# Two chunks of batch 1 instead of one are stored last with one-hot MoE rows; the second is computed among the last MoE stages

## The chip, the cores and the metric

The kernel runs on one core of one Trainium2 chip. The metric is the time of one execution on the device in microseconds. The kernel before took 265.82 us, the median of 12 runs (265.46 to 266.96). PE is the matrix engine, DVE the vector engine, ACT the scalar engine, POOL the GpSimd engine and SP the engine that only issues transfers here. PSUM is the memory that PE writes its results to; SBUF is the working memory.

## The reference

Inputs are q, k and v, each of 4 batches x 6208 rows x 256 columns, float32. The first half is an attention over columns (cross covariance), the second a mixture of depths (MoE): in each batch the 128 rows with the highest scores go through a small network and are replaced.

```
qn = q / (norm(q, axis=1) + 1e-6);  kn = k / (norm(k, axis=1) + 1e-6)
a  = softmax(kn.T @ qn / tau)           # 256 x 256 per batch, over the last axis
x  = v @ a                              # 6208 x 256 per batch
scores = x @ w_gate
for each batch b:
    top = the 128 rows of x[b] with the largest scores
    ye  = relu(x[b, top] @ w1) @ w2     # 256 -> 1024 -> 256
    g   = 1 / (1 + exp(-scores[b, top]))
    out[b, top] = x[b, top] + g * ye    # all other rows of out are x
```

The norm of every column needs all rows of q and k, so no row of the output of a batch can be computed before that batch's q and k have been read. The MoE rows of a batch are known only when all its scores are.

## The kernel before

**Tiling.** A batch is cut into six chunks of 1024 rows (0 to 5) and a rest of 64. A chunk lies in SBUF as 128 partitions x 8 rows x 256 columns. POOL's queue loads q, k and v, turning them to bf16 on the way. Batches are called by number, 0 to 3. In the code `H` is batch 1, `E` is batch 2 and `L` is batch 3.

**Stages of a batch.** `p1_steps` multiplies the rows of k with q into `s_ps` and collects the squares in `g_ps`. `softmax_stages` makes the 256 x 256 matrix `a_sb`, and a pair of columns `aw_sb`, with which scores can be had without x. Then, in groups of four rows of each partition, `p2_transpose` (op "T") transposes v into `vt_sb`, `p2_score` (op "S") adds the scores, and `p2_out` (op "O") multiplies with `a_sb` into a PSUM bank, two rows at a time, which ACT (late in the kernel also DVE) copies into an SBUF tile called `stage`. When a chunk's `stage` is full, `emit_store` issues a 1 MB store on SP's queue. `select_stages` finds the 128 rows by a search in seven steps on DVE and PE, and POOL gathers those rows of v by an indirect transfer (`vg`). `mlp_stages` transposes `vg`, forms the rows of x (`xe`), transposes them, runs the hidden layer (`h_sb`, 16 matmuls) and the output layer (8 matmuls), and makes the new rows, `upd`, on DVE. POOL then writes these 128 rows into the output by an indirect transfer, the scatter. It has to come behind the stores of the same batch, since it overwrites some of their rows, and it waits until they have landed.

**The order of the work.** The order of instructions on each engine is written out by hand: `plan` lists the operations, and generators for the softmax, the selection and the MoE (`smx_side`, `side`, `side2`) are advanced one stage at a time between them, by an estimate of the time spent (`spent`, `SLOT_US`). Output of batch b is computed among the first stage of batch b + 1. The last batch has no successor. While its q and k are loaded, batch 2's scores are computed and four groups of its output. Stores of batch 2, and those of batch 1's chunks 3 and 4 (`HOLD`), are held back in `deferred` and issued behind the last loads, by `flush_deferred`. Then come the rest of batch 2's output and batch 3's output, with batch 3's selection and batch 2's MoE between the pairs (`between`).

**A chunk that is stored last.** Batch 1's chunk 5 is treated otherwise. Its groups get only their scores in the usual place; their transposed rows wait in `vt_late`. Its output is computed between batch 3's softmax stages by `late_pair`, four times, two rows at a time. Each row takes two matmuls with `a_sb` and three more that add the MoE rows of that batch: a one-hot matrix made by `late_onehot` (which partition holds which chosen row) is multiplied with `late_parts`, the MoE's addition cut into three bf16 parts that sum to the float32 value. This chunk's store may thus come after batch 1's scatter. It is the last on SP's queue, issued behind all of batch 3's.

**The end.** After all output, the last MoE (batch 3's) runs by itself, behind 24 matmuls without a use for their result (`keep_warm`):

```
    emit_store(H, NFULL - 1)
    ...
    while waiting:
        side2.append(mlp_stages(waiting.pop(0)))
    keep_warm(24)
    while side2:
        advance(side2)
```

**Buffers.** There are seven `stage` tiles, so a chunk held back takes one away from the others. Most tiles of the MoE exist once or twice (`bufs`). PSUM banks are taken in turn by `out_psum`.

Of the kernel before, what the change touches and what calls it, by code (L numbers as in the profile page):

```python
# [9 lines left out]
F32 = mybir.dt.float32  # L10
BF16 = mybir.dt.bfloat16
# [3 lines left out]
ALU = mybir.AluOpType  # L15
AX = mybir.AxisListType

P = 128
RPP = 8
# [7 lines left out]
def kernel(  # L27
# [73 lines left out]
    gs = [g for ci in range(NFULL + 1) for g in groups(ci)]  # L101
    E = B - 2
    H = B - 3
    late = [(NFULL - 1, 0, 4), (NFULL - 1, 4, 4)]

    def mixed(b, ci, extra):

# [195 lines left out]
    def softmax_stages(b):  # L303
        s_ps, g_ps = acc[b]
        s_sb = smx.tile([P, 2, C], F32, name="s_sb")
        nc.scalar.copy(s_sb, s_ps)  # L306
        junk = smx.tile([P, P], F32, name="junk")
        nsq = smx.tile([P, 4], F32, name="nsq")
        for i in range(4):
            nc.vector.tensor_tensor_reduce(out=junk, in0=g_ps[:, i, :], in1=ident_f, scale=1.0,  # L310
                                           scalar=0.0, op0=ALU.mult, op1=ALU.add,
                                           accum_out=nsq[:, i:i + 1])


        y0 = smx.tile([P, 4], F32, name="y0")
        nc.vector.tensor_scalar(out=y0.bitcast(I32), in0=nsq.bitcast(I32), scalar1=-0.5,
                                scalar2=float(0x5F1FFFF9), op0=ALU.mult, op1=ALU.add)
        t0 = smx.tile([P, 4], F32, name="t0")
        nc.vector.tensor_tensor(out=t0, in0=nsq, in1=y0, op=ALU.mult)
        nc.vector.scalar_tensor_tensor(out=t0, in0=t0, scalar=-0.703952253, in1=y0, op0=ALU.mult,  # L320
                                       op1=ALU.mult)
        y1 = smx.tile([P, 4], F32, name="y1")
        nc.vector.scalar_tensor_tensor(out=y1, in0=t0, scalar=0.703952253 * 2.38924456, in1=y0,
                                       op0=ALU.add, op1=ALU.mult)
        x1 = smx.tile([P, 4], F32, name="x1")
        nc.vector.tensor_tensor(out=x1, in0=nsq, in1=y1, op=ALU.mult)
# [25 lines left out]
        a_sb = a_pool.tile([P, 2, C], BF16, name="a_sb")  # L352
        aw_sb = a_pool.tile([P, 2, 2], BF16, name="aw_sb")
        for cc in range(2):
            r = smx.tile([P, 1], F32, name=f"r{cc}")
            nc.vector.tensor_scalar_add(r, rsum[:, cc:cc + 1], 1e-9)
            nc.vector.reciprocal(r, r)
            nc.vector.tensor_scalar_mul(a_sb[:, cc, :], e[:, cc, :], r)
            awj = smx.tile([P, C], BF16, name="awj")
            nc.vector.tensor_tensor_reduce(out=awj, in0=a_sb[:, cc, :], in1=wg_bcast, scale=1.0,  # L360
                                           scalar=0.0, op0=ALU.mult, op1=ALU.add,
                                           accum_out=aw[:, cc:cc + 1])

        nc.vector.tensor_copy(aw_sb[:, :, 0], aw)
        nc.vector.tensor_tensor(out=aw_sb[:, :, 1], in0=aw, in1=aw_sb[:, :, 0], op=ALU.subtract)
        a_tiles[b] = (a_sb, aw_sb)
# [3 lines left out]
    stage_of = {}  # L370
    deferred = []
    gate_done = []
    held = {b: NFULL + 1 - (b == H) for b in range(B)}
    side = []
    side2 = []
    waiting = []
# [19 lines left out]
    def p2_transpose(b, g, on_act=False):  # L396
        ci, s0, n = g
        parts = P if ci < NFULL else REM
        vt = loaded[("v", b, ci)][0]
        vt_ps = vt_psum()  # L400
        for j in range(n):
            for cc in range(2):
                nc.tensor.transpose(vt_ps[:, cc, j, :parts], in_=vt[:parts, s0 + j, cc * P:(cc + 1) * P],  # L403
                                    identity=ident_b[:parts, :parts])
        if b == H and g in late:
            vt_sb = moe.tile([P, 2, 4, P], BF16, name="vt_late", bufs=2)
        else:
            vt_sb = vt_pool.tile([P, 2, 4, P], BF16, name="vt_sb")
        if on_act:
            nc.scalar.copy(vt_sb[:, :, :n, :parts], vt_ps[:, :, :n, :parts])  # L410
        else:
            nc.vector.tensor_copy(vt_sb[:, :, :n, :parts], vt_ps[:, :, :n, :parts])  # L412
        return vt_sb
# [74 lines left out]
    def late_pair(k):  # L488


        g = late[k // 2]
        onehot, parts = late_moe
        if k == 0:
            stage_of[(H, NFULL - 1)] = st_pool.tile([P, RPP, C], F32, name="stage")
        st = stage_of[(H, NFULL - 1)]
        a_sb = a_tiles[H][0]
        o_ps = out_psum()
        row = g[1] + k % 2 * 2
# [20 lines left out]

    def late_onehot(idx):  # L520

        base = float(H * N + (NFULL - 1) * CHUNK)
        at = moe.tile([P, 1], F32, name="late_at")
        nc.vector.tensor_copy(at, idx)
        nc.vector.tensor_scalar(out=at, in0=at, scalar1=-base, scalar2=1.0 / RPP, op0=ALU.add, op1=ALU.mult)
        at_row = moe.tile([P, RPP], F32, name="late_at_row")
        nc.vector.tensor_scalar(out=at_row, in0=iota_row[:, 0:RPP], scalar1=-1.0 / RPP, scalar2=at,
                                op0=ALU.mult, op1=ALU.add)
        onehot = moe.tile([P, RPP, P], BF16, name="late_onehot")
        nc.vector.tensor_tensor(out=onehot, in0=iota_row[:, None, :].to_broadcast([P, RPP, P]),  # L530
                                in1=at_row[:, :, None].to_broadcast([P, RPP, P]), op=ALU.is_equal)
        late_moe.append(onehot)

    def emit_store(b, ci):
# [13 lines left out]
    def select_stages(b):  # L548
# [85 lines left out]
        nc.vector.tensor_scalar(out=idx, in0=mps[:, NCOL + 2:NCOL + 3], scalar1=fl, scalar2=toff,  # L634
                                op0=ALU.max, op1=ALU.add)
        yield
        vg = moe.tile([P, C], BF16, name="vg", bufs=3)
        nc.gpsimd.indirect_dma_start(out=vg, out_offset=None, in_=v_flat,
                                     in_offset=bass.IndirectOffsetOnAxis(ap=idx[:, 0:1], axis=0))

# [5 lines left out]
    def mlp_stages(b):  # L646
# [2 lines left out]
        tp = ps_vt.tile([P, 2, 4, P], BF16, name="vt_ps")  # L649
        for cc in range(2):  # L650
            nc.tensor.transpose(tp[:, cc, 0, :], in_=vg[:, cc * P:(cc + 1) * P], identity=ident_b)
        vgt = moe.tile([P, 2, P], BF16, name="vgt", bufs=2)
        nc.vector.tensor_copy(vgt, tp[:, :, 0, :])
        yield
        mps = ps_m.tile([P, 512], F32, name="m_ps")
# [1 line left out]
            nc.tensor.matmul(mps[:, 0:C], lhsT=vgt[:, cc, :], rhs=a_sb[:, cc, :], start=cc == 0,  # L657
                             stop=cc == 1)
        xe = moe.tile([P, D], F32, name="xe", bufs=2)
        xe_b = moe.tile([P, D], BF16, name="xe_b", bufs=2)  # L660
        nc.vector.tensor_copy(xe_b, mps[:, 0:D])
        nc.vector.tensor_copy(xe, mps[:, 0:D])
        yield
        tp = ps_vt.tile([P, 2, 4, P], BF16, name="vt_ps")
        for dc in range(2):
            nc.tensor.transpose(tp[:, dc, 0, :], in_=xe_b[:, dc * P:(dc + 1) * P], identity=ident_b)
        xet = moe.tile([P, 2, P], BF16, name="xet", bufs=2)
        nc.vector.tensor_copy(xet, tp[:, :, 0, :])
        scj = moe.tile([P, D], BF16, name="scj")
        ssc = moe.tile([P, 1], F32, name="ssc")  # L670
        nc.vector.tensor_tensor_reduce(out=scj, in0=xe, in1=wg_bcast, scale=1.0, scalar=0.0, op0=ALU.mult,
                                       op1=ALU.add, accum_out=ssc)
        gate = moe.tile([P, 1], F32, name="gate", bufs=2)
        nc.scalar.activation(gate, ssc, AF.Exp, scale=-1.0)
        nc.vector.tensor_scalar_add(gate, gate, 1.0)
        nc.vector.reciprocal(gate, gate)
        yield
        h_sb = moe.tile([P, NFC, P], BF16, name="h_sb", bufs=2)
        for hf in range(NFC // 4):
            h_ps = out_psum().rearrange("p a c -> p (a c)")  # L680
            for f4 in range(4):
# [165 lines left out]
        do_out(E, op[2], False)  # L847
    for g in gs[-1:] + gs[:-1]:
        do_out(b, g, False)
    emit_store(H, NFULL - 1)  # L850
    while side:
        advance(side)
    while side2:
        advance_all(side2)
    while waiting:
        side2.append(mlp_stages(waiting.pop(0)))
    keep_warm(24)
    while side2:
        advance(side2)

# [34 lines left out]
```

## Time and profile before

| what | value |
|---|---|
| median of 12 runs | 265.82 us |
| the profiled execution's own time | 266.29 us |
| its span (first to last instruction) | 264.5 us |
| PE / DVE / ACT / POOL busy, share of the span | 76% / 46% / 31% / 21% |
| mean granted clock of PE | 0.94 |
| chain that ended last, by engine | DMA 59%, PE 16%, issue 11%, DVE 9% |
| DMA packets of the core | 66.97 MB, mean 253 GB/s |
| 1 MB stores, issue to landing (median of 24) | 8.9 us |
| scatters, issue to landing (median of 4) | 6.8 us |
| second to last and last scatter, start | 244.92 and 254.97 us |

Times inside the kernel are counted from the span's start. The span is shorter than the execution's time by what lies around it. The granted clock is the share of its full rate that PE got from its throttle. A row like `L477 PE MATMUL o_ps<-a_sb,vt_sb` names the line, the engine, the operation, and what is written from what. In the timeline the first two columns are the start and the time in which the row's instructions ran, and `xN` is how many they are; in brackets stands how long the engine had been idle and what ended that. In the chain of waits, each piece is an instruction, a transfer in flight (DMA), or time in which nothing that the profile shows was waited for ("issue"). `POOLq` and `SPq` are the sequencers of POOL and SP.

### The profile page before, as it was taken

How to read it: one execution, taken by the hardware profiler on the slowest of the kernel's cores; microseconds unless marked ns; L12 is line 12 of the kernel's file. 1: busy time of each engine (PE TensorE's matmuls, PEld its weight loads, DVE VectorE, ACT ScalarE, POOL GpSimd, SP SyncE). 2: the span in 40 equal slices, each digit the busy share in tenths (PEclk: the TensorE clock that was granted, in tenths of full speed). 3: DMA queues.
4: the chain of work that ended last, by engine and by line, in shares of the span. 5: the costliest groups of instructions: out<-in, count | busy, mean ns of one | idle time of the engine just before them, and what ended most of it. 6: DMA issues, size and time to landing. Idle time of an engine off the chain costs nothing.

```text
span 264.5 us, 6087 instructions
## 1 busy us (share of the span) xinstructions
PE 200.0 (76%) x2584; PEld 176.2 (67%) x2584; DVE 121.2 (46%) x464; ACT 81.7 (31%) x146; POOL 55.4 (21%) x104
## 2 busy tenths in 40 slices
PE   0096768899937677699986886899999799799700
PEld 0086656789926566589975785898988688578500
DVE  0200002614403366713438785773975827868400
ACT  3102000167720000118731000434102866795200
POOL 7113123121110023221301233320422003010110
PEclk9999999999977799799998899999999999999855
DMA  6999999999999999999999999999999989999960
GB/s 221 227 229 225 216 210 214 214 212 283 320 317 317 296 213 213 214 214 208 313 315 248 213 212 224 211 215 213 214 209 213 213 278 398 409 392 403 422 252 0
DMA packets 17642, 66.97 MB, mean 253 GB/s; under 512 B 2000, under 2 KB 4688, under 8 KB 14544
## 3 DMA queue, kind: packets, MB, share of 16 engines
q0 software_dynamic: 12384, 38.93, 73.7%
q1 hardware_dynamic: 5232, 27.66, 26.4%
q8 instruction: 20, 0.33, 0.4%
q14 instruction: 6, 0.05, 0.0%
HBM read 79.04 MB, written 25.95 MB: 397 GB/s over the span
## 4 chain that ended last, share of the span: by engine, by line
DMA 59%; PE 16%; issue 11%; DVE 9%; POOL 1%; ACT 1%; POOLq 1%; DVEq 0%; SPq 0%
DMA k_ch<-in_k_dram 26%; DMA v_ch<-in_v_dram 17%; DMA q_ch<-in_q_dram 13%; PE o_ps L477 5%; DMA out_dram<-stage 3%; PE s_ps L291 2%; PE vt_ps L403 2%; DVE cnt L588 2%; DVE cmp L584 2%; PE sc_ps L431 1%; PE g_ps L295 1%; PE g_ps L293 1%; DVE stage L483 1%; PE g_ps L477 1%; PE m_ps L595 1%
## 5 line engine op out<-in xcount | busy, mean ns | idle before, releaser
L291 PE MATMUL s_ps<-q_ch,k_ch 128*128 128x256 bf16 x384 | 95.1, 288 | 32.3 <-DMA k_ch<-in_k_dram 31.7
L293 PE MATMUL g_ps<-q_ch 128*128 128x128 bf16 x384 | 87.8, 229 | 1.1 <-DVE nsq L310 1.0
L295 PE MATMUL g_ps<-k_ch 128*128 128x128 bf16 x384 | 87.8, 229 | 0.0
L291 PEld LDWEIGHTS <-k_ch 128*128 128x128 bf16 x384 | 39.6, 103 | 37.8 <-DMA k_ch<-in_k_dram 34.9
L477 PE MATMUL o_ps<-a_sb,vt_sb 128*128 128x256 bf16 x298 | 43.9, 271 | 1.9 <-ACT vt_sb L410 1.3
L295 PEld LDWEIGHTS <-k_ch 128*128 128x128 bf16 x384 | 39.7, 103 | 8.0 <-issue 1.6
L485 ACT COPY stage<-o_ps 128x512 f32<-128x512 f32 x68 | 38.3, 590 | 15.5 <-PE o_ps L477 15.4
L293 PEld LDWEIGHTS <-q_ch 128*128 128x128 bf16 x384 | 39.6, 103 | 1.0 <-issue 0.6
L412 DVE COPY vt_sb<-vt_ps 128x1024 bf16<-128x1024 bf16 (+1 forms) x33 | 20.8, 633 | 31.7 <-PE vt_ps L403 31.6
L477 PEld LDWEIGHTS <-vt_sb 128*128 128x128 bf16 (+1 forms) x376 | 29.4, 97 | 8.1 <-issue 4.4
L403 PE MATMUL vt_ps<-ident_b,v_ch 128*128 128x128 bf16 x336 | 24.6, 219 | 1.8 <-DMA v_ch<-in_v_dram 0.7
L431 PEld LDWEIGHTS <-vt_sb 128*128 128x128 bf16 (+1 forms) x376 | 23.8, 96 | 2.5 <-DVE sc L552 0.2
L306 ACT COPY s_sb<-s_ps 128x512 f32<-128x512 f32 x4 | 2.3, 585 | 73.6 <-PE s_ps L291 43.0
L403 PEld LDWEIGHTS <-v_ch 128*128 128x128 bf16 x384 | 22.2, 97 | 4.0 <-DMA v_ch<-in_v_dram 3.0
L174 POOL DMA_DIRECT2D q_ch<-in_q_dram x23 | 12.7, 553 | 57.9 <-PE g_ps L295 35.9
L431 PE MATMUL sc_ps<-aw_sb,vt_sb 128*128 128x2 bf16 (+1 forms) x376 | 24.1, 164 | 0.0
L310 DVE CUSTOM_DVE_ANT_0 junk<-g_ps,ident_f 128x128 f32<-128x128 f32 x16 | 4.6, 290 | 38.7 <-PE g_ps L295 38.3
L174 POOL DMA_DIRECT2D v_ch<-in_v_dram x24 | 12.8, 538 | 25.0 <-DMA q_ch<-in_q_dram 12.2
L174 POOL DMA_DIRECT2D k_ch<-in_k_dram x23 | 12.5, 543 | 25.4 <-DMA k_ch<-in_k_dram 7.6
L588 DVE TENSOR_REDUCE cnt<-cmp 128x7 bf16<-128x343 bf16 x28 | 14.4, 513 | 1.0
L410 ACT COPY vt_sb<-vt_ps 128x1024 bf16<-128x1024 bf16 x11 | 10.6, 1012 | 13.1 <-PE vt_ps L403 13.1
L584 DVE SCALAR_TENSOR_TENSOR cmp<-u,delta,shares 128x343 bf16<-128x343 f32 x24 | 13.9, 579 | 0.9
(156 smaller groups left out, 215.0 us busy)
## 6 DMA issues: line engine op xcount, KB each, us to landing
out_dram<-stage SPq DMA_DIRECT2D x24, 1024.0 KB, 8.9
v_ch<-in_v_dram POOLq DMA_DIRECT2D x24, 512.0 KB, 14.8
q_ch<-in_q_dram POOLq DMA_DIRECT2D x23, 512.0 KB, 16.9
k_ch<-in_k_dram POOLq DMA_DIRECT2D x23, 512.0 KB, 17.9
stage<-in_moe_w_dram SPq DMA_DIRECT2D x2, 1024.0 KB, 23.4
q_ch<-in_q_dram POOLq DMA_DIRECT2D x2, 256.0 KB, 9.6
k_ch<-in_k_dram POOLq DMA_DIRECT2D x2, 256.0 KB, 9.7
out_dram<-stage_rem SPq DMA_DIRECT2D x4, 64.0 KB, 20.5
```

The source lines that it names most:

```text
L174: ins = nc.gpsimd.dma_start(out=t, in_=view(src, b, ci))
L291: nc.tensor.matmul(s_ps[:, cc, :], lhsT=ks[:, sl], rhs=qs, start=first and cc == 0, stop=last and cc == 1)
L293: nc.tensor.matmul(g_ps[:, cc, :], lhsT=qs[:, sl], rhs=qs[:, sl], start=first and cc == 0, stop=False)
L295: nc.tensor.matmul(g_ps[:, 2 + cc, :], lhsT=ks[:, sl], rhs=ks[:, sl], start=False, stop=last and cc == 1)
L403: nc.tensor.transpose(vt_ps[:, cc, j, :parts], in_=vt[:parts, s0 + j, cc * P:(cc + 1) * P], identity=ident_b[:parts, :parts])
L410: nc.scalar.copy(vt_sb[:, :, :n, :parts], vt_ps[:, :, :n, :parts])
L412: nc.vector.tensor_copy(vt_sb[:, :, :n, :parts], vt_ps[:, :, :n, :parts])
L431: nc.tensor.matmul(sc_ps[:parts, col, :], lhsT=vt_sb[:, cc, j, :parts], rhs=aw_sb[:, cc, :], start=cc == 0 and col in (0, NCOL - 1), stop= ...
L477: nc.tensor.matmul(o_ps[:parts, pj, :], lhsT=vt_sb[:, cc, j, :parts], rhs=a_sb[:, cc, :], start=pj == 0 and cc == 0, stop=pj == m - 1 and ...
L485: nc.scalar.copy(st[:parts, s0 + pair * 2:s0 + pair * 2 + m, :], o_ps[:parts, :m, :])
L584: nc.vector.scalar_tensor_tensor(out=cmp, in0=wide, scalar=delta, in1=thr, op0=ALU.subtract, op1=ALU.is_ge)
L588: nc.vector.tensor_reduce(out=cnt, in_=cmp, axis=AX.X, op=ALU.add)
```

## The change

Batch 1's chunks 4 and 5 are now both treated as chunk 5 was. Their four groups get only scores in their usual place among batch 2's first stage, and chunk 4 is no longer in the list of stores held back. `late_onehot` makes two one-hot matrices. The four `late_pair` operations between batch 3's softmax stages now compute chunk 4, and its store is issued where that of chunk 5 was. Chunk 5 is computed in the last MoE: two pairs in place of the `keep_warm` matmuls, one after the stage that makes `xe`, one after the hidden layer; its store follows. To make room, several tiles lose a buffer, and some results that nobody reads share one.

```diff
-    late = [(NFULL - 1, 0, 4), (NFULL - 1, 4, 4)]
+    LATE = [NFULL - 2, NFULL - 1]
+    late = [(ci, s0, 4) for ci in LATE for s0 in (0, 4)]
...
-        junk = smx.tile([P, P], F32, name="junk")
+        junk = smx.tile([P, P], BF16, name="junk")
...
-            awj = smx.tile([P, C], BF16, name="awj")
+            awj = smx.tile([P, C], BF16, name="junk_row")
...
-    held = {b: NFULL + 1 - (b == H) for b in range(B)}
+    held = {b: NFULL + 1 - (len(LATE) if b == H else 0) for b in range(B)}
...
-            vt_sb = moe.tile([P, 2, 4, P], BF16, name="vt_late", bufs=2)
+            vt_sb = moe.tile([P, 2, 4, P], BF16, name="vt_late", bufs=len(late))
...
-        onehot, parts = late_moe
-        if k == 0:
-            stage_of[(H, NFULL - 1)] = st_pool.tile([P, RPP, C], F32, name="stage")
-        st = stage_of[(H, NFULL - 1)]
+        onehots, parts = late_moe
+        onehot = onehots[:, LATE.index(g[0]), :, :]
+        if g[1] == 0 and k % 2 == 0:
+            stage_of[(H, g[0])] = st_pool.tile([P, RPP, C], F32, name="stage")
+        st = stage_of[(H, g[0])]
...
-        onehot = moe.tile([P, RPP, P], BF16, name="late_onehot")
-        nc.vector.tensor_tensor(out=onehot, in0=iota_row[:, None, :].to_broadcast([P, RPP, P]),
-                                in1=at_row[:, :, None].to_broadcast([P, RPP, P]), op=ALU.is_equal)
+        onehot = moe.tile([P, len(LATE), RPP, P], BF16, name="late_onehot")
+        for i in range(len(LATE)):
+            at_row = moe.tile([P, RPP], F32, name=f"late_at_row{i}")
+            nc.vector.tensor_scalar(out=at_row, in0=iota_row[:, 0:RPP], scalar1=-1.0 / RPP, scalar2=at,
+                                    op0=ALU.mult, op1=ALU.add)
+            nc.vector.tensor_tensor(out=onehot[:, i, :, :], in0=iota_row[:, None, :].to_broadcast([P, RPP, P]),
+                                    in1=at_row[:, :, None].to_broadcast([P, RPP, P]), op=ALU.is_equal)
+            if i + 1 < len(LATE):
+                nc.vector.tensor_scalar(out=at, in0=at, scalar1=-float(P), scalar2=None, op0=ALU.add)
...
-        vg = moe.tile([P, C], BF16, name="vg", bufs=3)
+        vg = moe.tile([P, C], BF16, name="vg", bufs=2)
...
-        h_sb = moe.tile([P, NFC, P], BF16, name="h_sb", bufs=2)
+        h_sb = moe.tile([P, NFC, P], BF16, name="h_sb")
...
-    emit_store(H, NFULL - 1)
+    emit_store(H, LATE[0])
     while side:
         advance(side)
     while side2:
         advance_all(side2)
-    while waiting:
-        side2.append(mlp_stages(waiting.pop(0)))
-    keep_warm(24)
+    late_pair(4)
+    late_pair(5)
+    side2.append(mlp_stages(waiting.pop(0)))
+    advance(side2)
+    advance(side2)
+    late_pair(6)
+    advance(side2)
+    advance(side2)
+    late_pair(7)
+    emit_store(H, LATE[1])
     while side2:
         advance(side2)
```

`vgt`, `xe_b`, `xet` and `gate` also go from two buffers to one, like `h_sb`, and `scj` shares the tile `junk_row` with `awj`. The instructions of POOL keep their order. On PE, some stages of the selection and the MoE stand one or two steps later among the matmuls of batch 2's and batch 3's first stage, since less time is counted as spent before them.

More of the change, by code (lines that the diff above doesn't have):

```diff
@@ L520, in late_onehot @@
     def late_onehot(idx):
-        base = float(H * N + (NFULL - 1) * CHUNK)
+        base = float(H * N + LATE[0] * CHUNK)
         at = moe.tile([P, 1], F32, name="late_at")
@@ L525, in late_onehot @@
         nc.vector.tensor_scalar(out=at, in0=at, scalar1=-base, scalar2=1.0 / RPP, op0=ALU.add, op1=ALU.mult)
-        at_row = moe.tile([P, RPP], F32, name="late_at_row")
-        nc.vector.tensor_scalar(out=at_row, in0=iota_row[:, 0:RPP], scalar1=-1.0 / RPP, scalar2=at,
-                                op0=ALU.mult, op1=ALU.add)
-        onehot = moe.tile([P, RPP, P], BF16, name="late_onehot")
-        nc.vector.tensor_tensor(out=onehot, in0=iota_row[:, None, :].to_broadcast([P, RPP, P]),
-                                in1=at_row[:, :, None].to_broadcast([P, RPP, P]), op=ALU.is_equal)
+        onehot = moe.tile([P, len(LATE), RPP, P], BF16, name="late_onehot")
[7 more added lines that the diff above has]
+                nc.vector.tensor_scalar(out=at, in0=at, scalar1=-float(P), scalar2=None, op0=ALU.add)
         late_moe.append(onehot)
@@ L651, in mlp_stages @@
             nc.tensor.transpose(tp[:, cc, 0, :], in_=vg[:, cc * P:(cc + 1) * P], identity=ident_b)
-        vgt = moe.tile([P, 2, P], BF16, name="vgt", bufs=2)
+        vgt = moe.tile([P, 2, P], BF16, name="vgt")
         nc.vector.tensor_copy(vgt, tp[:, :, 0, :])
@@ L659, in mlp_stages @@
         xe = moe.tile([P, D], F32, name="xe", bufs=2)
-        xe_b = moe.tile([P, D], BF16, name="xe_b", bufs=2)
+        xe_b = moe.tile([P, D], BF16, name="xe_b")
         nc.vector.tensor_copy(xe_b, mps[:, 0:D])
@@ L666, in mlp_stages @@
             nc.tensor.transpose(tp[:, dc, 0, :], in_=xe_b[:, dc * P:(dc + 1) * P], identity=ident_b)
-        xet = moe.tile([P, 2, P], BF16, name="xet", bufs=2)
+        xet = moe.tile([P, 2, P], BF16, name="xet")
         nc.vector.tensor_copy(xet, tp[:, :, 0, :])
-        scj = moe.tile([P, D], BF16, name="scj")
+        scj = smx.tile([P, D], BF16, name="junk_row")
         ssc = moe.tile([P, 1], F32, name="ssc")
@@ L672, in mlp_stages @@
                                        op1=ALU.add, accum_out=ssc)
-        gate = moe.tile([P, 1], F32, name="gate", bufs=2)
+        gate = moe.tile([P, 1], F32, name="gate")
         nc.scalar.activation(gate, ssc, AF.Exp, scale=-1.0)
```

## The prediction

> **What bounds the kernel now.** I read the page's rows by slice first, to see which resource is full in which stage:
>
> ```profile
> PEclk9999999999977799799998899999999999999855
> DMA  6999999999999999999999999999999989999960
> GB/s 221 227 229 225 216 210 214 214 212 283 320 317 317 296 213 213 214 214 208 313 315 248 213 212 224 211 215 213 214 209 213 213 278 398 409 392 403 422 252 0
> ```
>
> A slice is 6.6 us. The DMA engines are full, but for a dip in the 33rd or 34th, from the second slice to the 38th. To slice 32 (some 212 us) they mostly load, at 213 GB/s. After it they only store, at about 400 GB/s. In the last slice nothing moves, yet the kernel has not ended. Which work ends last is answered by the chain of waits, in order of time, and by the list of what POOL waited for:
>
> ```profile
> 245.03 0.70 DVE stage L483
> 245.79 8.27 DMA out_dram<-stage
> 254.21 0.54 issue
> 254.75 1.19 POOLq L890
> ...
> POOL out_dram L707 <- DMA out_dram<-stage: 9.1, 1, 9.1
> ...
> L890 POOLq DRAIN  x3: 51/97/8944, 254.7 to 264.2; - x3
> ```
>
> Batch 3's last chunk is copied by DVE at 245.03 and its store is issued at 245.79; the store flies for 8.27 us, to 254.06. POOL's indirect scatter of batch 3's MoE rows has waited for it (9.1 us), and starts 0.9 us later. POOL's drain at the program's end takes 8.94 us and finishes at 263.7, so what matters is when this scatter can start. The last rows of the timeline tell what else it needs:
>
> ```profile
> 244.39 0.60 PE L477 MATMUL g_ps<-a_sb,vt_sb 128*128 128x256 bf16 x4
> 244.83 1.50 PE L419 MATMUL o_ps<-ones_b,ident_b 128*128 128x128 bf16 x24
> 246.17 0.28 PE L651 MATMUL vt_ps<-ident_b,vg 128*128 128x128 bf16 x2
> 246.83 0.39 PE L657 MATMUL m_ps<-a_sb,vgt 128*128 128x256 bf16 x2 [0.39 <-DVE vgt L653]
> 247.74 0.28 PE L666 MATMUL vt_ps<-ident_b,xe_b 128*128 128x128 bf16 x2 [0.52 <-DVE xe_b L661]
> 248.41 0.62 PE L684 MATMUL o_ps<-xet,w_sb 128*128 128x128 bf16 x8 [0.39 <-DVE xet L668]
> 249.72 1.89 PE L692 MATMUL o_ps<-w_sb,h_sb 128*128 128x256 bf16 x8 [0.24 <-ACT h_sb L687]
> 251.65 0.48 DVE L701 SCALAR_TENSOR_TENSOR upd<-o_ps,gate,xe 128x256 f32<-128x256 f32 x1 [2.33 <-PE o_ps L692]
> 254.97 0.97 POOL L707 DMA_INDIRECT out_dram<-upd,idx  x1 [9.07 <-DMA out_dram<-stage]
> ```
>
> Its data, `upd`, is ready at 252.13, 2.84 us before the scatter starts. So the last MoE has slack and the queue of stores has none.
>
> **The store queue.** SP's stores after the last loads are, before: batch 1 chunks 3 and 4, batch 2 chunks 0 to 5, two short ones, batch 3 chunks 0 to 5, batch 1 chunk 5. The change takes chunk 4 of batch 1 out of second place and puts it where chunk 5 was, with chunk 5 behind it. The bytes stay, but one store less stands ahead of batch 3's last. Each 1 MB store costs about 2.6 us of the DMA engines: 1.05 MB at about 400 GB/s, slices 34 to 37. Without it, batch 3's last store would land at 254.06 - 2.6 = 251.5, provided the queue doesn't run dry. Its issue stays at 245.79, since copies set it, so 5.7 us would be left in flight. A 1 MB store with nothing ahead would take some 2.6 + 2.4 = 5.0 us (an estimate; 2.4 us is the flight of the last scatter, whose queues were nearly empty). So the queue is still loaded, if barely. The scatter's two other waits on transfers: batch 2's scatter flies 7.3 us from 244.92, to 252.2. With 0.9 us to get going, stores allow a start at 252.4, that scatter at 253.1.
>
> **The last MoE.** PE gets 40 matmuls of 128x256 there: four pairs of rows, each 4 ordinary and 6 one-hot matmuls. The first four such pairs are in the trace:
>
> ```profile
> 212.66 0.38 PE L501 MATMUL o_ps<-a_sb,vt_late 128*128 128x256 bf16 x2
> 212.88 0.49 PE L504 MATMUL o_ps<-late_parts,late_onehot 128*128 128x256 bf16 x3
> 213.21 0.38 PE L501 MATMUL o_ps<-a_sb,vt_late 128*128 128x256 bf16 x2
> ```
>
> A row comes every 0.55 us, a pair every 1.09. Step by step, with the offsets between the rows above:
> - Two pairs stand in place of the 24 warming matmuls (244.83 to 246.17, 1.34 us): the transposes start at 244.83 + 2.18 = 247.01 (+0.84). The gathered rows landed 8.4 us after their issue at 236.92, at 245.3, so they don't hold it.
> - The matmul for xe follows 0.66 later, at 247.67. Pair 6 then holds PE from 247.89 to 248.98. The transposes of xe_b would be due at 247.67 + 0.91 = 248.58, so 0.40 is lost.
> - The hidden layer comes 0.67 later, at 249.65, and its 16 matmuls end at 250.56. Pair 7 holds PE to 251.65, where the old offset (1.31) gives 250.96: 0.69 lost.
> - The last 8 matmuls. In the row above they run at a granted clock of 0.50, 1.93 us from first start to `upd`; for batch 2, at full clock, it is 1.08 (243.08 to 244.16). With pairs in PE's gaps I take 1.08: 0.85 gained. `upd` runs 252.73 to 253.21; the scatter starts 0.28 later, as batch 2's did (244.64 to 244.92): 253.5.
>
> Sum: +0.84 + 0.40 + 0.69 - 0.85 = +1.08 on `upd`. The start is the latest of 252.4, 253.1 and 253.5: 253.5 against 254.97, or **1.5 us earlier**. The MoE chain becomes the last wait. The four copies on ACT (0.59 us each) lie in gaps of 0.6 us and more: pair 6's ends at 249.8, before the gate (250.0), pair 7's follows the hidden layer's.
>
> The clock is the disputed price. From 249.65 it is 0.50, after 3.4 us in which PE streamed columns for 0.34 of the time (the matmuls that the timeline shows there, at 0.055 us per 128 columns). Counted so, the stretches of 3.4 us from 246.2 on would hold 0.65 to 0.85 after the change; those between 220 and 246 us hold 0.56 to 0.97 and ran at full clock. The Trainium skill, "TensorE: Matmul & The Clock Gate", section "HAM oscillation — how this bites in real kernels", speaks of idle gaps above some 3.4 us as what halves the clock. The rows above show PE idle for 0.52 us at most at a time, and it halved all the same, so here the trace decides. By the page alone neither version would be halved, and the scatter would still start at 253.5. If the clock halves again, the hidden layer ends at 251.37, pair 7 at 253.52, `upd` at 255.9 and the scatter starts at 256.2: 1.2 later than before. These are the bounds, -1.5 and +1.2. I take -1.5.
>
> **What I cost at nothing.** In batch 2's phase 16 matmuls and 4 copies go (4 x 0.44 us of PE), but PE waits for loads there; no gain. The second one-hot is 1.22 us of DVE at 157.7 (row of the first) and two tiny instructions, before batch 2's softmax. DMA is full there and loads are issued 14.8 to 17.9 us before they land (medians of the issue rows), so a late PE finds its data waiting and catches up; if that cover failed, up to 1.5 us. Side stages slip by one slot of 1.7 us on PE; the MoE parts of batch 1, ready at 192.3, are needed at 204.4. Fewer buffers (vg, h_sb and others): their readers belong to a batch that has finished. POOL's order of instructions is unchanged. Batch 1's scatter waits for one store less; on SP the moved chunk 4 waits for that scatter, landed at 228, and only chunk 5 stands behind it. Chunk 5 is issued at some 252.5 and lands by some 257.5, before the drain's end.
>
> **Which end counts.** The drain starts with the scatter, and no run here shows whether it lasts 8.94 us from there or 6.3 us from the landing at 257.4. By the first the kernel gains 1.5 us. By the second the landing counts: the scatter flies 2.4 us in empty queues, 7.3 in full ones, so it lands between 255.9 and 260.8 (-1.5 to +3.4). But all stores are written by about 256.5, so I expect 256.5 to 257, a gain of 0.4 to 0.9. I take the first, since the drain's record begins at the scatter's start.
>
> The profiled execution took 266.29 us for a span of 264.5, 0.47 over the median 265.82. By its sum it would take 264.8; on the median, 264.35.
>
> **Rivals.**
> - The end follows the landing: 264.9 to 265.4. For it: 6.3 of the drain's 8.94 us come after the landing, and something must fill them. Against: the record starts before the scatter, as if it only ran out.
> - The scatter is held by two later stores sharing its DMA engines (other side). It needs the drain tied to the landing and a landing after 257.4, 3.9 us in flight. Batch 2's took 7.3. At +0.5 to +1 (stores drained by 257.5 or later): 266.3 to 266.8.
> - The halved clock, or pairs that cost more: it decides once `upd` ends after 254.7, 1.5 us later than I have it; at half clock 267.0.
> - The queue of stores runs dry, and batch 3's last lands as late as ever: nothing is gained, 265.8. For it: 5.7 against 5.0 us. Against: full DMA in every window from 216 to 254.
> - The load phase stretches, its cover failing: up to 1.5 us, so 265.9 with the gain.
>
> **How the numbers follow.** A measurement of this kernel tells 0.2% (0.53 us) from no change. Chances: as worked out 0.52 (264.35, own range 263.7 to 265.0); end by landing 0.18 (two thirds of it faster); queue dry or cover failing 0.08 (same); late landing 0.08, halved clock or dear pairs 0.09, something else 0.05, all slower. Faster 0.64, same 0.14, slower 0.22. The range reaches from 263.6 to the rivals at 266.8.
>
> **What would show it.** Right: POOL's last scatter waits for DVE `upd`, no longer for a store; batch 3's last store lands near 251.5; clock 1.0 to 252; the drain still some 8.9 us. Wrong: PE clock 0.50 during pair 7; a flight of 4 us or more for the last scatter with the end behind it; last loads landing after 216.

## The result and the profile after

The changed kernel takes 264.64 us (median of 10 runs, 264.45 to 265.66), the kernel before 265.88 us beside it on the same chip (40 runs, 265.46 to 266.96). The ratio is 0.9954, with a 95% interval of 0.9944 to 0.9964: 1.24 us faster. The forecast was 264.35 us. The profiled execution of the changed kernel took 264.57 us for a span of 262.9; that of before took 266.29 for 264.5.

The page's rows by slice, again 6.6 us each:

```profile
PEclk9999799999998799799987899999999999999995
GB/s 217 228 230 228 217 213 210 215 213 277 317 316 320 301 216 215 213 212 211 301 319 258 214 211 224 213 212 213 216 206 214 214 281 352 421 394 374 418 367 2
```

Two things differ from before. The granted clock is 9 tenths or more in slices 38 and 39, where it was 8 and then 5. And slices 34 and 37, where there are only stores, move 352 and 374 GB/s instead of 398 and 403: the DMA engines now have pauses. The chain of waits in order of time, the list of what POOL waited for, and the drain:

```profile
244.90 0.70 DVE stage L484
245.66 6.52 DMA out_dram<-stage
252.42 0.69 issue
253.10 1.20 POOLq L902
...
POOL out_dram L712 <- DVE upd L706: 14.6, 2, 7.6
...
L902 POOLq DRAIN  x3: 51/97/8952, 253.1 to 262.6; - x3
```

The chain still names batch 3's last store, with a flight of 6.52 us instead of 8.27. But the scatter waits no longer for it: in POOL's list the scatters wait for DVE's `upd`, twice, and the longer wait, 7.6 us, is the last scatter's. (The chain follows the sequencer, which was through with the store at 252.42; POOL itself waited 0.9 us longer.) The drain is as long as before, 8.95 us, and begins 1.65 us earlier. The rows of the timeline (start, busy time):

```profile
244.70 0.38 PE L503 MATMUL o_ps<-a_sb,vt_late 128*128 128x256 bf16 x2
246.88 0.28 PE L656 MATMUL vt_ps<-ident_b,vg 128*128 128x128 bf16 x2
247.54 0.39 PE L662 MATMUL m_ps<-a_sb,vgt 128*128 128x256 bf16 x2 [0.39 <-DVE vgt L658]
247.77 0.38 PE L503 MATMUL o_ps<-a_sb,vt_late 128*128 128x256 bf16 x2
248.87 0.28 PE L671 MATMUL vt_ps<-ident_b,xe_b 128*128 128x128 bf16 x2
249.52 0.61 PE L689 MATMUL g_ps<-xet,w_sb 128*128 128x128 bf16 x8 [0.38 <-DVE xet L673]
250.41 0.38 PE L503 MATMUL s_ps<-a_sb,vt_late 128*128 128x256 bf16 x2
251.50 1.04 PE L697 MATMUL o_ps<-w_sb,h_sb 128*128 128x256 bf16 x8
252.58 0.48 DVE L706 SCALAR_TENSOR_TENSOR upd<-o_ps,gate,xe 128x256 f32<-128x256 f32 x1 [2.15 <-PE o_ps L697]
253.34 0.97 POOL L712 DMA_INDIRECT out_dram<-upd,idx  x1 [7.57 <-DVE upd L706]
```

The four pairs of chunk 5 stand where the forecast had them: two ahead of the transposes (244.70 to 246.88), one behind the matmul for xe (from 247.77), one behind the hidden layer (from 250.41). The last 8 matmuls take 1.04 us instead of 1.89, since the clock is whole. `upd` is ready at 253.06, 0.93 us later than before, and the scatter starts at 253.34, 1.63 us earlier than before. The slack has changed sides: the store landed at 252.18, and with the 0.9 us that POOL needed after a store before, that one would have let the scatter start at about 253.1 (at 253.2 with the 1.0 us that it takes in the versions below). The MoE is the last wait by some 0.2 us only.

### The profile page after: what moved, and what is told of

Its sections match the earlier page's. It is cut to its first block, busy times and chain, and to the rows that moved or that the text cites. A ratio compares the mean times of both kernels' runs of the same rounds, so it can differ in the third digit from the quotient of the medians.

```text
span 262.9 us, 6092 instructions
## 1 busy us (share of the span) xinstructions
PE 202.1 (77%) x2584; PEld 178.6 (68%) x2584; DVE 122.9 (47%) x467; ACT 81.8 (31%) x146; POOL 55.6 (21%) x104
## 4 chain that ended last, share of the span: by engine, by line
DMA 54%; PE 19%; issue 13%; DVE 8%; POOL 2%; ACT 1%; POOLq 1%; DVEq 0%; SPq 0%
DMA k_ch<-in_k_dram 23%; DMA q_ch<-in_q_dram 17%; DMA v_ch<-in_v_dram 11%; PE o_ps L478 5%; PE s_ps L292 4%; DMA out_dram<-stage 2%; PE vt_ps L404 2%; PE g_ps L296 2%; PE g_ps L294 2%; DVE cnt L593 1%; DVE cmp L589 1%; PE sc_ps L432 1%; DVE junk L311 1%; DVE stage L484 1%; PE m_ps L343 1%
## 5 line engine op out<-in xcount | busy, mean ns | idle before, releaser
L292 PE MATMUL s_ps<-q_ch,k_ch 128*128 128x256 bf16 x384 | 96.1, 290 | 33.1 <-DMA k_ch<-in_k_dram 32.4
L478 PE MATMUL o_ps<-a_sb,vt_sb 128*128 128x256 bf16 x282 | 41.5, 271 | 1.9 <-ACT vt_sb L411 1.3
L486 ACT COPY stage<-o_ps 128x512 f32<-128x512 f32 x64 | 36.1, 589 | 14.0 <-PE o_ps L478 14.0
L478 PEld LDWEIGHTS <-vt_sb 128*128 128x128 bf16 (+1 forms) x360 | 28.4, 97 | 8.1 <-issue 4.4
L413 DVE COPY vt_sb<-vt_ps 128x1024 bf16<-128x1024 bf16 (+1 forms) x31 | 19.3, 631 | 27.7 <-PE vt_ps L404 27.6
L432 PEld LDWEIGHTS <-vt_sb 128*128 128x128 bf16 (+1 forms) x360 | 22.3, 96 | 2.4 <-DVE gate L680 0.2
L432 PE MATMUL sc_ps<-aw_sb,vt_sb 128*128 128x2 bf16 (+1 forms) x360 | 22.6, 164 | 0.1
L311 DVE CUSTOM_DVE_ANT_0 junk<-g_ps,ident_f 128x128 bf16<-128x128 f32 x16 | 4.6, 290 | 37.4 <-PE g_ps L296 37.0
```

Source lines behind the costliest of these rows:

```text
L292: nc.tensor.matmul(s_ps[:, cc, :], lhsT=ks[:, sl], rhs=qs, start=first and cc == 0, stop=last and cc == 1)
L432: nc.tensor.matmul(sc_ps[:parts, col, :], lhsT=vt_sb[:, cc, j, :parts], rhs=aw_sb[:, cc, :], start=cc == 0 and col in (0, NCOL - 1), stop= ...
L478: nc.tensor.matmul(o_ps[:parts, pj, :], lhsT=vt_sb[:, cc, j, :parts], rhs=a_sb[:, cc, :], start=pj == 0 and cc == 0, stop=pj == m - 1 and ...
L486: nc.scalar.copy(st[:parts, s0 + pair * 2:s0 + pair * 2 + m, :], o_ps[:parts, :m, :])
```

## The experiments

The theory: the order of the stores brought the gain, by releasing the scatter from the queue; the pairs among the MoE stages are dearer than the warming matmuls on a path that had slack, and are paid with the scatter only as far as they outlast the queue; the program ends a fixed time after the last scatter's start. The rivals: the gain is from the pairs or from the warming matmuls that went, or the end follows the last scatter's landing. All ratios are against the kernel before, beside it on the same chip.

### The order of the last stores alone

Everything of the change is kept, but chunk 4 of batch 1 is stored ahead of all of batch 3's chunks, so that as many stores stand ahead of batch 3's last one as before.

```diff
+    emit_store(H, LATE[0])
     for g in gs[-1:] + gs[:-1]:
         do_out(b, g, False)
     ...
-    emit_store(H, LATE[0])
```

> The changed kernel, with the store of batch 1's chunk 4 issued ahead of all of batch 3's stores instead of behind them. Everything that is computed keeps its place. Theory (the gain is the store order): batch 3's last store has one store more ahead of it again, lands near 254 instead of 252.2, the last scatter waits for it and starts near 254.9, and the time is that of the kernel before within 0.3 us (265.6 to 266.0). Rival (the gain comes from the last MoE, where matmuls of chunk 5 keep the clock up and replace the warming ones): the time stays at that of the changed kernel, 264.6.

It took 266.33 us, ratio 1.0029 (1.0002 to 1.0055). Batch 3's last store in its chain, and the scatter's row in its timeline:

```profile
245.75 8.37 DMA out_dram<-stage
...
255.04 0.97 POOL L712 DMA_INDIRECT out_dram<-upd,idx  x1 [9.17 <-DMA out_dram<-stage]
```

Batch 3's last store landed at 254.12, and the scatter waits for it again. The whole gain is gone, and 0.3 us with it, while the pairs, the lost warming matmuls and the smaller pools are all still there. So the gain is the order's.

### The other half alone: all pairs early, the order kept

Here chunk 4 and chunk 5 are both computed between batch 3's softmax stages, both stores come behind batch 3's, and the last MoE runs behind the 24 warming matmuls as before.

```diff
-    W = [("late", H, k) for k in range(4)]
+    W = [("late", H, k) for k in range(8)]
...
     emit_store(H, LATE[0])
     ...
-    late_pair(4)
-    late_pair(5)
-    side2.append(mlp_stages(waiting.pop(0)))
-    ...
-    late_pair(7)
     emit_store(H, LATE[1])
+    side2.append(mlp_stages(waiting.pop(0)))
+    keep_warm(24)
```

> The order of the stores alone: chunk 4 and chunk 5 of batch 1 are both computed by the eight pairs between batch 3's softmax stages, the 24 warming matmuls stand ahead of the last MoE as before, and both stores follow batch 3's. Theory: four more pairs (4.4 us of PE) stand where batch 3's last chunk of v has just landed, and push all that follows by some 4 us: batch 3's last store is issued near 249.7, the MoE's result is ready near 256, the scatter starts near 256.3: 267 to 268, slower than both. Rival (the place of chunk 5's pairs doesn't matter, the order is all): 264.6.

It took 267.99 us, ratio 1.008 (1.0059 to 1.0101), 3.4 us more than the changed kernel:

```profile
249.31 6.31 DMA out_dram<-stage
...
254.45 0.48 DVE L706 SCALAR_TENSOR_TENSOR upd<-o_ps,gate,xe 128x256 f32<-128x256 f32 x1 [1.60 <-PE o_ps L697]
256.63 0.97 POOL L712 DMA_INDIRECT out_dram<-upd,idx  x1 [7.20 <-issue]
```

The four pairs on PE push batch 3's output back: its last store is issued at 249.31, 3.65 us later than in the changed kernel, and lands at 255.63. That store held the scatter, which starts 1.0 us after it (its row names no releaser), and not `upd`, which was ready at 254.93, a microsecond earlier than expected. The order brings something only if the work taken out of the way goes to a place where nobody waits for it; put between batch 3's softmax stages as here, the four pairs did not find one.

### The warming matmuls

Taken out of the kernel before, with nothing in their place (`keep_warm(24)` deleted):

> The kernel before without the 24 warming matmuls ahead of the last MoE. Theory (before, stores bind and the last MoE has 2.8 us of slack): the MoE starts up to 1.3 us earlier and its result waits longer; the scatter starts at 255.0 as before and the time is unchanged, 265.9 within 0.3 us. Rival (the chain of the last MoE sets the end): 1.0 to 1.3 us faster, or slower where the clock halves a window earlier.

It took 265.71 us, ratio 0.9991 (0.9974 to 1.0008): no difference. The MoE starts earlier, runs its last matmuls at half clock, and its result then waits 3.4 us for the store:

```profile
248.75 1.86 PE L692 MATMUL o_ps<-w_sb,h_sb 128*128 128x256 bf16 x8 [0.24 <-ACT h_sb L687]
250.65 0.48 DVE L701 SCALAR_TENSOR_TENSOR upd<-o_ps,gate,xe 128x256 f32<-128x256 f32 x1 [2.29 <-PE o_ps L692]
254.48 0.97 POOL L707 DMA_INDIRECT out_dram<-upd,idx  x1 [8.73 <-DMA out_dram<-stage]
```

Added to the changed kernel, ahead of its MoE (`keep_warm(24)` behind `late_pair(5)`):

> The changed kernel with 24 warming matmuls (1.34 us of PE) put back ahead of the last MoE, behind the two pairs of rows. Theory (after the change the chain of the last MoE binds, with 0.2 us to spare over the stores): the last scatter starts 1.3 us later, at 254.7, and the time rises by 1.1 to 1.4 us, to 265.7 to 266.0. Rival (the stores still bind): unchanged, 264.6.

It took 266.11 us, ratio 0.9999 (0.9981 to 1.0017). Its profiled execution was its longest (267.95 us): PE's granted clock was 0.50 in the windows from 218 to 224, and everything behind them is 2 us late, so only a length inside it is used: from the first of the four pairs to the scatter it is 256.72 - 246.74 = 9.98 us, where the changed kernel has 253.34 - 244.70 = 8.64.

```profile
246.74 0.38 PE L503 MATMUL o_ps<-a_sb,vt_late 128*128 128x256 bf16 x2
256.72 0.97 POOL L712 DMA_INDIRECT out_dram<-upd,idx  x1 [8.91 <-DVE upd L706]
```

The 1.34 us are the length that the 24 matmuls had before (244.83 to 246.17), and they reach the end whole: 1.2 us by the ratios. Before, the same matmuls cost nothing. The two runs together say which path was last: the queue before the change, the MoE after it.

### How far the MoE is the bound

If the MoE is last by only 0.2 us, making it shorter must bring next to nothing. In the first of three versions all four pairs of chunk 5 come behind the MoE's matmuls:

```diff
-    late_pair(4)
-    late_pair(5)
     side2.append(mlp_stages(waiting.pop(0)))
-    advance(side2)
-    ...
-    late_pair(7)
+    for _ in range(5):
+        advance(side2)
+    for k in range(4, 8):
+        late_pair(k)
     emit_store(H, LATE[1])
```

> The changed kernel with chunk 5's four pairs of rows all behind the last MoE's matmuls on PE, none ahead of them or between. Theory (pairs cost the MoE chain 1.9 us, but stores stand only 0.2 us behind it): the MoE's result is ready near 250.5, the last scatter waits for batch 3's last store again (landed at 252.2) and starts near 253.1, so only 0.1 to 0.4 us are gained, 264.2 to 264.6; with PE less busy the clock halves during the MoE's last matmuls, and chunk 5's store is issued near 256. Rival (the pairs are the whole price, stores no longer bind): 2 us or more faster, 262.6. Second rival (pairs between the stages were needed for the clock): chunk 5's store so late that the end waits for it, slower than 265.6.

It took 264.47 us, ratio 0.9945 (0.9926 to 0.9965), not to be told from the changed kernel.

```profile
249.91 0.48 DVE L706 SCALAR_TENSOR_TENSOR upd<-o_ps,gate,xe 128x256 f32<-128x256 f32 x1 [1.58 <-PE o_ps L697]
252.93 0.97 POOL L712 DMA_INDIRECT out_dram<-upd,idx  x1 [7.16 <-issue]
```

`upd` comes 2.67 us earlier than in the changed kernel, and the scatter 0.41: it starts 1.0 us after batch 3's last store, landed at 251.93, and the view of that store names the scatter as what waited for it (7.2 us). The time came out as expected, but not all of the way there: the clock was expected to halve, and stayed at 1.00 while PE worked, so that chunk 5's store was issued at 254.89.

The second splits two of the pairs into rows (`late_row` is half of `late_pair`), which go into PE's gaps between the MoE stages, with the other two pairs behind:

```diff
-    late_pair(4)
-    late_pair(5)
     side2.append(mlp_stages(waiting.pop(0)))
-    ...
+    for k, pj in ((4, 0), (4, 1), (5, 0), (5, 1)):
+        advance(side2)
+        late_row(k, pj)
     advance(side2)
     late_pair(6)
     late_pair(7)
     emit_store(H, LATE[1])
```

> The changed kernel with chunk 5's first two pairs cut into single rows (0.55 us of PE each), one in each gap of the last MoE where PE waits for DVE or ACT (0.55 to 0.9 us from first start to first start); the other two pairs stand behind the MoE's matmuls. Theory: nothing is added to the MoE chain and the clock stays at 1.0, its result is ready near 250.0, 3 us earlier; the stores then bind and the scatter starts near 253.1, 264.2 to 264.6. Rival (the MoE chain alone binds): 262 or less. The difference between this and the pairs behind the MoE is the clock.

It took 264.36 us, ratio 0.9937 (0.9917 to 0.9957), and `upd` was ready at 250.56, 2.5 us earlier than in the changed kernel. The scatter started at 253.27, behind a store that landed at 252.26. Run side by side on one chip, it and the changed kernel were level:

> The changed kernel once more, beside the version with rows in the gaps on the same chip. Ratio to the kernel before 0.9945 to 0.9965, as measured.

> Rows in the gaps once more, beside the changed kernel. If its gain over the changed kernel is real it is what its last scatter starts earlier: stores allow a start at 253.1 to 253.3 where the MoE chain of the changed kernel gave 253.3, so 0 to 0.3 us faster than it. Rival (the pairs in the MoE chain cost all they add to it): 1 us or more faster than the changed kernel.

The changed kernel took 264.67 us (0.9954, 0.9940 to 0.9968), the version with rows 264.58 us (0.9965, 0.9945 to 0.9986). The third also moves chunk 4's last pair into a gap, so that chunk 4's store is issued at 247.68 instead of 246.08 and has less to do with batch 3's last; the last three pairs of chunk 5 stand behind the MoE:

```diff
-    W = [("late", H, k) for k in range(4)]
+    W = [("late", H, k) for k in range(3)]
...
+    for k, pj in ((3, 0), (3, 1), (4, 0), (4, 1)):
+        advance(side2)
+        late_row(k, pj)
+        if (k, pj) == (3, 1):
+            emit_store(H, LATE[0])
```

> As the run with rows in the gaps, but chunk 4's last pair is computed in the first two gaps too, so that chunk 4's store is issued some 2 us later (near 248 instead of 246). Theory (batch 3's last store waits for what stands ahead of it in the queue, not for what stands behind): it lands near 252 as before, time as in the run with rows in the gaps within 0.2 us. Rival (chunk 4's store shares the engines with it and delays it): it lands near 251, the scatter starts near 252, 263.2 to 263.6.

Its median was 265.37 us, ratio 0.9984 (0.9952 to 1.0015), so the expected time was missed: five of its ten runs lie between 264.10 and 264.80 us, five between 265.95 and 267.84. The cause of the spread stays open. In its profiled execution (264.42 us) batch 3's last store landed at 252.20, as in the changed kernel (252.18), after a flight of 6.30 us against 6.52; the version with all pairs behind, with chunk 4's store issued 0.4 us behind batch 3's last one, has 6.28. So a store issued 0.4 us behind it does not slow it measurably.

So the new bound lies just behind the old one. Shortening the MoE by 2.5 us is worth nothing that can be measured, since the store's landing, at about 252, holds the scatter at about 253. No version here beats the changed kernel measurably.

### What the end waits for

An extra load, which nothing reads, is queued on SP behind the last store, so that the last scatter shares the DMA engines with 1 MB more:

```diff
     emit_store(H, LATE[1])
+    spare = st_pool.tile([P, RPP, C], F32, name="stage")
+    nc.sync.dma_start(out=spare, in_=view(q, 0, 0))
```

> The changed kernel with one more transfer: behind the last store, SP loads 1 MB of q into a free stage tile that nobody reads. It keeps the DMA engines busy while the last scatter flies. Theory (the end is the drain of 8.95 us that starts with the scatter's issue): the scatter lands 0.5 to 2.5 us later, the drain still takes 8.95 us, the time stays at 264.6 within 0.3 us. Rival (the drain ends a fixed 4.8 us after the scatter's landing): the time rises as much as the landing is late, to 265.1 to 267.1.

It took 266.67 us, ratio 1.002 (1.0006 to 1.0035), 2.0 us more than the changed kernel by the medians and 1.8 by the ratios. Its scatter started at 253.18, 0.16 earlier than in the changed kernel, and landed at 260.05, 2.7 later; the drain lasted 10.99 us:

```profile
L904 POOLq DRAIN  x3: 51/97/10992, 252.9 to 264.5; - x3
...
DMA to landing us min/median/max: 6.9/6.9/6.9
```

So the theory of a drain with a fixed length fell. But the end doesn't simply follow the landing either, since the kernel before and the changed one have their last landing at the same time, 257.40 and 257.33, and end 1.6 us apart:

```profile
DMA to landing us min/median/max: 2.4/2.4/2.4
```

```profile
DMA to landing us min/median/max: 4.0/4.0/4.0
```

(the first line is the last scatter's flight before, the second that in the changed kernel.) A rule fits all three: the drain ends 8.95 us after its start, or 3.9 us after the scatter has landed, whichever is later. Half the load (`spare[:, 0:4, :]`, 0.5 MB) tries it between the two:

> The changed kernel with a load of 0.5 MB behind the last store, half of what the earlier run loaded. It makes the last scatter land near 258.7, between the two earlier cases (257.33: drain 8.95 us; 260.05: drain 10.99 us). Theory (the drain ends at the later of two times, 8.95 us from its start or 3.9 us from the scatter's landing): it ends near 262.6, drain 9.2 to 10, time 265.0 to 265.7. Rival (the drain's length depends on the transfers after it, not on the landing): 264.6 or 266.7.

It took 265.7 us, ratio 0.9994 (0.9968 to 1.002). The drain lasted 9.62 us:

```profile
L904 POOLq DRAIN  x3: 51/97/9616, 253.0 to 263.1; - x3
```

| kernel | drain starts | scatter lands | drain lasts | it ends, after its start / after the landing |
|---|---|---|---|---|
| before | 254.75 | 257.40 | 8.944 | 8.94 / 6.3 |
| changed | 253.10 | 257.33 | 8.952 | 8.95 / 4.7 |
| all pairs early | 256.41 | 260.83 | 8.941 | 8.94 / 4.5 |
| 0.5 MB behind | 253.00 | 258.73 | 9.616 | 9.62 / 3.9 |
| 1 MB behind | 252.95 | 260.05 | 10.992 | 10.99 / 3.9 |

The rule was written ahead of the half load's run, and holds in it. What the drain does in its 8.95 us, or in the 3.9, no run shows. In the changed kernel the landing could have come 0.8 us later (257.33 + 3.9 = 261.2, against 262.05) at no cost.

## Why the prediction was right, and where it was off

**What bounds the kernel**: right. Restoring the order alone took the whole gain back.

**The last MoE**: right, step by step. The tail began 0.13 us earlier than in the profiled execution of before; with that taken off, every step stands within 0.03 us of its forecast:

| step | forecast | measured | difference |
|---|---|---|---|
| transposes of `vg` | 247.01 | 246.88 | -0.13 |
| matmul for xe | 247.67 | 247.54 | -0.13 |
| transposes of `xe_b` (end of pair 6) | 248.98 | 248.87 | -0.11 |
| hidden layer | 249.65 | 249.52 | -0.13 |
| last 8 matmuls (end of pair 7) | 251.65 | 251.50 | -0.15 |
| `upd` | 252.73 | 252.58 | -0.15 |
| scatter | 253.5 | 253.34 | -0.16 |

**The clock**, named as the disputed price: it stayed at 1.00 to 254, as taken. The prediction's count, the share of time in which PE streams columns over 3.4 us, got this right. In two kernels the clock halved while the MoE's matmuls still ran. The 3.4 us up to the halving had a share of 0.34 (before) and 0.38 (before, without the warming matmuls), and in each PE was idle for 0.52 us at most at a time. With all pairs behind the MoE the share is 0.56 in two such stretches in a row, and the clock held. Here are two windows of that run, then the one of the run without warming matmuls in which it is down (length, busy time on PE, its weight loads, DVE, ACT and POOL, granted clock, DMA share, GB/s):

```profile
247.00:249.00 2.00, 1.31 (x19) 1.09 (x18) 0.98 (x6) 1.08 (x3) 0.00 (x0) 1.00 1.03 422
249.00:251.00 2.00, 2.00 (x20) 1.67 (x18) 0.48 (x1) 0.21 (x1) 0.00 (x0) 1.00 1.00 418
```

```profile
249.00:251.00 2.00, 1.61 (x8) 0.82 (x6) 0.35 (x1) 0.18 (x1) 0.00 (x0) 0.50 1.03 432
```

With all pairs early, the same MoE runs behind the same 24 warming matmuls as before, with nothing in PE's gaps, and its last 8 matmuls take 1.10 us, not 1.89:

```profile
253.31 1.10 PE L697 MATMUL o_ps<-w_sb,h_sb 128*128 128x256 bf16 x8 [0.30 <-ACT h_sb L692]
```

There the stretches, counted back from the clock's next change at 257.09, fall so that one of them (250.26 to 253.67) holds half of these 8 matmuls too, which makes its share 0.47, and the clock held. So whether such an MoE is halved also depends on where the stretches fall. The share is no sharp rule either: earlier in the traces a stretch of 0.38 held (before, 160.90 to 164.31), and one of 0.43 was followed by a halved clock (all pairs early, 103.49 to 106.90).

The Trainium skill, "TensorE: Matmul & The Clock Gate", section "HAM oscillation — how this bites in real kernels", makes idle gaps above some 3.4 us the cause of a halved clock. These runs halve it with no gap near that length, so as a sufficient sign of safety the rule does not hold here. A long gap is followed by a halved clock too: with chunk 4 ahead of batch 3, PE's last matmul ends at 252.64 and the clock halves at 256.09.

**The store queue**: the mechanism was right, the size off. The step that fell short is its proviso, "provided the queue doesn't run dry", taken as met since "the queue is still loaded, if barely". Of the 2.6 us that one store less should have been worth, 1.9 arrived: batch 3's last store landed at 252.18, not 251.5. Two readings of the trace bear on it. The queue did run dry, in the windows 220:224 and 238:240, first before, then after:

```profile
220.00:222.00 2.00, 1.81 (x19) 1.53 (x17) 1.22 (x8) 0.62 (x2) 0.92 (x2) 1.00 1.00 406
222.00:224.00 2.00, 1.70 (x17) 1.38 (x16) 1.64 (x6) 1.93 (x4) 0.77 (x1) 1.00 1.01 406
238.00:240.00 2.00, 2.00 (x22) 1.80 (x20) 1.97 (x5) 1.21 (x3) 0.00 (x0) 1.00 1.05 434
```

```profile
220.00:222.00 2.00, 1.81 (x18) 1.56 (x16) 1.25 (x6) 0.75 (x2) 1.57 (x2) 1.00 0.88 333
222.00:224.00 2.00, 1.71 (x17) 1.38 (x16) 1.64 (x6) 1.90 (x5) 0.00 (x0) 1.00 0.86 294
238.00:240.00 2.00, 2.00 (x22) 1.81 (x20) 2.00 (x6) 1.21 (x3) 0.00 (x0) 1.00 0.83 285
```

At 220 to 224 some 0.37 MB are missing (2 us x 73 GB/s + 2 us x 112 GB/s), 0.9 us at 410 GB/s. This shortfall belongs to no order of the last stores: the run with chunk 4 ahead of batch 3 shows it too (301 GB/s in the mean of these four microseconds). It fits stores that began earlier (the first at 212.79 instead of 214.02) and of which three, not four, stand ahead of the one issued at 222.35. The first store waits for the second to last load of v, whose last part landed at 212.77, against 214.00 before; why that part is later in the two profiles without the change (213.48 in the other) and in none of the eleven with it (212.4 to 212.9) stays open. At 238 to 240 it is 0.3 MB, 0.7 us, and the run with chunk 4 ahead of batch 3 does not have this one (422 GB/s), but is 50 GB/s lower in the window before (364 against 414). Over both windows, 236 to 240, the changed kernel is 0.17 MB behind it, 0.4 us.

The time at which the middle ones of a store's sixteen parts landed tells where the loss lies. Batch 3's second store came 2.8 us earlier than before (239.4 against 242.2), its third 2.2 us (242.8 against 245.0), its last 2.2. So up to the second store the whole 2.6 us had arrived, the first dry stretch being made up by the earlier start, and some 0.5 us went at the second. At batch 3's last store the queue was indeed loaded: it flew for 6.52 us, where a store with nothing ahead takes 3.9, not the estimated 5.0 (all pairs behind: chunk 5's, issued at 254.89 with chunk 4's landed at 254.35, lands at 258.74). The prediction looked at that store alone, and the queue ran dry before it, at 238 to 240.

The other reading: a 1 MB store lands in sixteen parts, and the last of them is late. Fifteen parts of batch 3's last store had landed by 251.29, the median at 250.5; the sixteenth came at 252.18. Before, the median was 252.7 and the last 254.06. So the parts' median came 2.2 us earlier, their last 1.9. This would make it 0.4 us for the dry queue and 0.3 for the late part; no run takes one of them away alone. It cost next to nothing, because the MoE had become the later of the two.

Batch 2's scatter, named as the next floor (252.2), landed at 250.35 and held nothing.

**Cost at nothing**: nearly right. With the order restored, what is left of the change cost 0.3 us (ratio 1.0002 to 1.0055), and no run shows which part of it. The last loads of v landed at 216.2 against 216.0. Chunk 5's store was issued at 252.31 (forecast 252.5) and landed at 257.03 (257.5), and its cover was the drain.

**Which end counts**: right in its result, and too simple as a rule. The prediction chose between two ends; both exist, and the later one rules. The rival of a late landing came nearer than its 0.08 suggests. The last scatter did fly 4.0 us instead of 2.4, for the very reason that rival gave, and 0.8 us more would have made it count. The two loads put behind it are that rival made real, at +1.1 and +1.8 us by the ratios.

**The size of the gain**: 1.63 us on the scatter's start in the two profiles, forecast 1.5, but 1.24 between the medians. The forecast took its 1.5 us off the median, though it had noted that the profiled execution of before lay 0.47 us above it. That execution's last store was late; in the run of before without warming matmuls (265.71 us) the scatter starts at 254.48, not 254.97, behind the same store, after a first store issued at 213.50, not 214.02. The gain counted from an unusually long execution is too large by about that.

## What to carry to other kernels

Where the program's last act waits for the end of a full queue, what counts is the work that stands in that queue ahead of the thing waited for; whatever nobody waits for may go behind it, down to the time that the end of the program takes anyway, as long as the computation moved finds a free place too. Before you take a saving from such a queue, look at what would be last next: here the two floors lay 0.2 us apart, and a further 2.5 us saved on one of them brought nothing. Take differences from executions near the median, or say by how much yours is away from it.

## What the runs showed that was not expected

- The drain of POOL at the program's end has two conditions: 8.94 to 8.95 us from its start (in eleven profiles), and 3.9 us after the last scatter's landing (twice, 9.62 and 10.99 us).
- The flight of a scatter of 128 rows depends on what shares the DMA engines: 2.4 us behind the tail of one store, 4.0 with a 1 MB store issued 1.0 us ahead of it, 5.5 and 6.9 with 0.5 and 1 MB more behind that.
- The clock halved in the MoE at a streaming share of 0.34 and 0.38 over 3.4 us with no gap on PE above 0.52 us, and held at 0.47 and 0.56. Elsewhere in the traces the two sides overlap (held at 0.38, halved at 0.43).
- The last of the sixteen parts of a 1 MB store lands 0.4 to 2.0 us after the median part (1.3 in batch 3's last store before, 1.7 after the change), and the store counts as landed only then.
